# Activations transposed by VectorE and carried through DRAM, in place of TensorE transposes: an attention and mixer block on one core

## The chip, the core and the metric

The kernel runs on one core of a Trainium2 chip. The core has five engines, each with its own instruction stream: TensorE (PE) for matmuls, VectorE (DVE), ScalarE (ACT), GpSimd (POOL) and SyncE (SP), which here issues the DMAs. Data is computed on in SBUF (128 partitions); matmuls write PSUM. DRAM is reached by DMA. The metric is the device time of one execution in microseconds; the median of three runs of the kernel before is 1322.94 us (1322.71 to 1323.16).

## The reference

x has S = 2048 tokens of D = 576 channels, F = 4608 is the hidden width. Attention (32 heads of 18 channels, each token looking at itself and seven tokens at steps of two before it) and a mixer block both read the normalized x, and are added to x.

```python
def _A_ref(x, wqkv, wo):
    qkv = transpose((x @ wqkv).reshape(B, S, 3, H, Dh), 2, 0, 3, 1, 4)
    ...
    attn = _softmax(logits, axis=-1)
    o = einsum("bhsw,bhswd->bhsd", attn, vg)
    return transpose(o, 0, 2, 1, 3).reshape(B, S, D) @ wo

def _B_ref(x, w1, w2, w3, w4):
    h = _gelu(_layernorm(x) @ w1)
    ...                       # four channel groups shifted by +1, -1, +2, -2 tokens
    hs = concatenate([g0, g1, g2, g3], axis=-1) @ w2
    x1 = x + hs
    h2 = _gelu(_layernorm(x1) @ w3) @ w4
    return x1 + h2

xn = _layernorm(x)
return x + _A_ref(xn, wqkv, wo) + _B_ref(xn, w1, w2, w3, w4)
```

## The kernel before

**Matmuls.** Operands are split into two parts of a shorter float format, hi and lo (ACT rounds to hi, DVE subtracts to get lo). A product over 576 channels is 14 matmuls (`PAIRS`, L35): three for each of four chunks of 128 channels (hi·hi, hi·lo, lo·hi), and two for the last 64 channels, whose hi and lo share one chunk ("the tail"). An activation block that PE reads is thus `xt` of shape 128 x 9 x 512: channel on the partition, nine slices (0 to 3 hi, 4 the tail with hi in rows 0 to 63 and lo in rows 64 to 127, 5 to 8 lo), 512 tokens. Two such blocks live in `ring`, two more in `xp`.

**Transposing.** Layernorm and residual work has the token on the partition (16 tiles of 128 tokens, `Y[:, t, :]`), so each tile must be turned. `transposes` (L97) does it: four PE transposes (L102) of 128 x 128, for every second tile one more for two tiles' tails (L105), into a PSUM tile of the pool psb; ACT copies hi out (L107, L110), DVE makes lo (L111, L114). It is called for the normalized x (`prep_x`), for z, the layernorm of that again (`z_prep`, L146), for the layernorm of x1 (`n_prep`, L473), and for the attention output o (`prep_o`, L688).

**Stages, in PE's order.** Every engine runs its instructions in program order.
- Q: q, k, v for 16 tiles (`q_half`, L236), spilled to DRAM (`qkvd`).
- Mix (loop at L422): for each of four 512-token blocks b four tiles of W1 columns (`mix_tile`) and a remainder (`mix_rem`), whose 16-row groups are exchanged by eight small DMAs v<-u (L400, L401); pieces of work from `todo` then place them in T4 (L414). z of block b+1 is prepared meanwhile. W2 is loaded (`load_w2`, its tails by eight DMAs, L370) and split here.
- W2 (L481): 16 tiles; after each DVE adds to Y (L495) and takes statistics (`stats`: L88 to L90 on DVE, the power of -1/2 on POOL, L91). x1's layernorm of tiles 0 to 7 is prepared here, of 8 to 15 in units 0 to 2 (`LATE`, L645).
- The MLP: 72 units u = (c, b) of two hidden chunks and one block (L697). A unit is two `up` (14 matmuls, two gelus on ACT, lo on DVE) and four `down` of the unit before (12 matmuls, addition to Y on DVE, L639). `up` uses two PSUM buffers (psa), `down` three (psb). Attention runs in pieces on DVE in the background (`bg`) and stores o to DRAM (`od`, L554).
- The o stage (L743 to L767): the last four downs, then 16 tiles of o times Wo. o is read back two tiles at a time (`load_o`), turned and split one tile at a time.

All DMAs are issued by SP in program order, and an instruction whose data are not ready holds those behind it.

## Time and profile before

| | |
|---|---|
| median of three runs | 1322.94 us |
| the profiled execution | 1322.94 us |
| its span in the trace | 1321.2 us |
| DMA, share of 16 engines | 24%, 92.6 MB |
| under 512 B | 73504 of 120325 packets |
| granted TensorE clock | 1.0 |

The profile is of one execution. The span runs from the first to the last record; "busy" is an engine's time in instructions. A group row gives a program line, engine, operation, tiles and shapes, its count, then busy time and mean duration of one in ns, then idle time before. A row of a timeline gives start and length in us.

### The profile page before, as it was taken

What the parts mean: (1) busy time and instruction counts of PE and PEld (TensorE: products, weight loads), DVE (VectorE), ACT (ScalarE), POOL (GpSimd) and SP (SyncE); (2) the same over time, 40 slices, a digit from 0 to 9 for tenths busy, and PEclk for the clock granted to TensorE, in tenths of its full rate; (3) what the DMA queues carried; (4) which work ended last, traced back from release to release, by engine and by line L of the source; (5) the groups of instructions that cost most, each with busy time, mean ns of one, the idle gap of its engine ahead of it and who ended that gap; (6) DMA issues with size and microseconds to landing.
All of it is one profiled execution on the core that took longest, in us unless ns stands there. A gap on an engine that the chain in (4) does not pass through costs nothing.

```text
span 1321.2 us, 18855 instructions
## 1 busy us (share of the span) xinstructions
PE 1312.1 (99%) x7894; PEld 1208.0 (91%) x7894; DVE 921.9 (70%) x1332; ACT 348.2 (26%) x633; POOL 35.2 (3%) x92
## 2 busy tenths in 40 slices
PE   8999999999999999999999999999999999999998
PEld 8999998899899999999999999999999999999998
DVE  6443326687676778878868868878877886884454
ACT  4322225411423222222122222223213223122111
POOL 2010100011000000000000000000000000000000
PEclk9999999999999999999999999999999999999999
DMA  7644322020112021221221220220320200212164
GB/s 211 152 107 108 98 68 69 18 82 28 59 30 80 20 71 39 71 71 39 71 71 29 80 71 20 90 71 20 90 71 19 82 28 20 71 42 95 46 192 140
DMA packets 120325, 93.76 MB, mean 71 GB/s; under 512 B 73504, under 2 KB 100000, under 8 KB 120240
## 3 DMA queue, kind: packets, MB, share of 16 engines
q1 hardware_dynamic: 120240, 92.56, 23.9%
q8 instruction: 62, 1.02, 0.3%
q14 instruction: 23, 0.19, 0.0%
HBM read 67.83 MB, written 23.66 MB: 69 GB/s over the span
## 4 chain that ended last, share of the span: by engine, by line
PE 96%; DVE 2%; ACT 1%; SPq 1%; issue 1%; DMA 0%; POOL 0%; DVEq 0%; ACTq 0%; POOLq 0%
PE ps L636 34%; PE p L616 34%; PE ps L133 18%; PE ps L230 3%; PE p L380 3%; PE ps L102 2%; PE p L272 0%; PE p L395 0%; PE p L764 0%; DVE bn L88 0%; PE ps L105 0%; ACT xt L107 0%; DVE xt L111 0%; SPq L370 0%; DVE xt L114 0%
## 5 line engine op out<-in xcount | busy, mean ns | idle before, releaser
L636 PE MATMUL ps<-W,hi 128*128 128x288 f32 x2304 | 397.9, 294 | 0.5 <-DVE oT L114 0.5
L636 PEld LDWEIGHTS ps<-W,hi 128*128 128x128 f32 x2304 | 339.5, 188 | 6.1 <-PE ps L102 0.7
L620 ACT ACTIVATE hi<-p 128x512 fp32r<-128x512 f32 x144 | 86.2, 599 | 619.3 <-PE p L616 619.3
L636 PE MATMUL ps<-W,lo 128*128 128x288 f32 x1152 | 245.3, 294 | 0.0
L616 PE MATMUL p<-xt,W 128*128 128x512 f32 x1008 | 235.4, 390 | 0.0
L616 PE MATMUL p<-x1n,W 128*128 128x512 f32 x1008 | 234.9, 389 | 0.0
L622 DVE TENSOR_TENSOR lo<-g,hi 128x512 fp32r<-128x512 f32 x144 | 99.7, 692 | 193.2 <-ACT g L621 193.2
L639 DVE TENSOR_TENSOR Y<-ps,Y 128x576 f32<-128x576 f32 x288 | 212.8, 751 | 16.3 <-PE ps L636 16.1
L616 PEld LDWEIGHTS p<-x1n,W 128*128 128x128 f32 x1008 | 187.2, 188 | 36.8
L616 PEld LDWEIGHTS p<-xt,W 128*128 128x128 f32 x1008 | 187.1, 188 | 36.9
L636 PEld LDWEIGHTS ps<-W,lo 128*128 128x128 f32 x1152 | 185.4, 187 | 0.0
L133 PE MATMUL ps<-WQ,xt 128*128 128x432 f32 x672 | 135.3, 360 | 0.0
L133 PEld LDWEIGHTS ps<-WQ,xt 128*128 128x128 f32 x672 | 125.2, 188 | 5.2
L111 DVE TENSOR_TENSOR xt<-ps,xt 128x512 fp32r<-128x512 f32 x40 | 27.6, 689 | 87.2 <-ACT xt L110 52.1
L568 DVE TENSOR_TENSOR prod<-q,k 128x1152 f32<-128x1152 f32 x64 | 86.5, 1351 | 0.0
L571 DVE TENSOR_REDUCE L<-prod 128x64 f32<-128x1152 f32 x64 | 86.2, 1347 | 0.0
L621 ACT ACTIVATE g<-p 128x512 f32<-128x512 f32 x144 | 85.4, 593 | 0.0
L548 DVE TENSOR_TENSOR prod<-v,L 128x1152 f32<-128x1152 f32 x56 | 75.6, 1350 | 0.0
L552 DVE TENSOR_TENSOR o<-o,prod 128x1152 f32<-128x1152 f32 x56 | 75.6, 1350 | 0.0
L118 ACT CAST W<-rawf 128x640 fp32r<-128x640 f32 x72 | 50.5, 702 | 68.9 <-PE ps L636 62.2
L133 PE MATMUL ps<-Wo,oT 128*128 128x288 f32 x420 | 59.1, 298 | 0.2
L133 PEld LDWEIGHTS ps<-Wo,oT 128*128 128x128 f32 x420 | 56.2, 188 | 1.4 <-issue 1.4
(103 smaller groups left out, 941.9 us busy)
## 6 DMA issues: line engine op xcount, KB each, us to landing
qkvd<-stg SPq DMA_DIRECT2D x24, 432.0 KB, 3.4
rawf<-in_B_w_dram SPq DMA_DIRECT2D x36, 288.0 KB, 3.0
rawf<-in_B_w_dram SPq DMA_DIRECT2D x36, 256.0 KB, 2.9
xin<-in_A_x_dram SPq DMA_DIRECT2D x16, 288.0 KB, 3.8
q<-qkvd SPq DMA_DIRECT2D x8, 576.0 KB, 3.8
k<-qkvd SPq DMA_DIRECT2D x8, 576.0 KB, 5.7
v<-qkvd SPq DMA_DIRECT2D x8, 576.0 KB, 5.9
od<-o SPq DMA_DIRECT2D x8, 576.0 KB, 4.9
```

The source lines that it names most:

```text
L118: act.copy(dst_hi, raw)
L133: pe.matmul(ps[:, h, :n], xs(a), ws(b, h), start=i == 0, stop=i == len(PAIRS) - 1)
L548: dve.tensor_tensor(dst, vv, Lf[:, :, w:w + 1].to_broadcast([128, TPP * GH, HD]), op=ALU.mult)
L552: dve.tensor_tensor(o, o, dst, op=ALU.add)
L568: dve.tensor_tensor(prod.rearrange("p (j h) d -> p j (h d)", h=GH), q, k[:, r0:r0 + TPP, :], op=ALU.mult)
L571: dve.tensor_reduce(Lf[:, :, w], prod, axis=AX.X, op=ALU.add)
L616: pe.matmul(ps, W3[f][:, w, :], x1n[b][:, a, :], start=n == 0, stop=n == len(PAIRS) - 1)
L620: act.activation(hi, ps, AF.Gelu_apprx_tanh)
L621: act.activation(g32, ps, AF.Gelu_apprx_tanh)
L622: dve.tensor_tensor(lo, g32, hi.bitcast(F32), op=ALU.subtract)
L636: pe.matmul(ps[:, k, :HF], h[:, col], w[:, p, k * HF:(k + 1) * HF], start=n == 0, stop=n == len(seq) - 1)
L639: dve.tensor_tensor(yv, ps[:, :, :HF], yv, op=ALU.add)
```

## The change

z, the layernorm of x1, and o are no longer transposed by PE. Per tile, `turn` lets DVE transpose 32 x 32 pieces into a buffer `ST` (512 channels in one instruction, the 64 of the tail twice in another). After four tiles `put` writes ST to DRAM by four DMAs, one for every 32 partitions, such that rows come to lie by channel; `get` reads the block into the slices 4 to 8 of `xt` by two DMAs; `split_x` makes hi and lo of it (ACT and DVE). Columns of a block then lie in another order of tokens (32-token groups first), which the gelus undo by reading PSUM in a permuted order (`in_order`, `by_token`); o is read from DRAM in the matching order (`quads`), four tiles at a time into one buffer.

The work is put at other places: z is turned in Q after second halves of tiles 6 to 13; its blocks are fetched and split at tiles 12 and 14, at the end of Q, and within mix; x1's layernorm (its norm now on POOL) is turned at W2's tiles 2 to 5, 9, 10, 13 and 14 and, for the last four tiles, in unit 0. Its blocks are fetched at tiles 8 and 13 and in units 0 and 1, and split at tiles 11 and 15 and in units 1 and 2. o is turned after the downs of units 68 to 71, fetched from unit 69 on, and split in units 70 and 71, after the last downs, and at tile 5 of the o stage. The attention is finished one unit earlier (u = 67). In mix, matmuls write PSUM tiles of psb instead of psa, block 3 starts with its remainder, and the loads and splits of W2 and the pieces of `todo` come at other steps.

```diff
...
-    def norm(dst, src, kind, t):
-        dve.tensor_scalar(dst, src, MV[kind][:, t, 0:1], RS[kind][:, t, 1:2],
+    def norm(dst, src, kind, t, eng=dve):
+        eng.tensor_scalar(dst, src, MV[kind][:, t, 0:1], RS[kind][:, t, 1:2],
                           op0=ALU.subtract, op1=ALU.mult)
 
...
@@ -114,6 +112,53 @@
...
+    def room(p):
+        nonlocal ST, RT
+        ST = p.tile([128, 20, 128], F32, name="st")
+        RT = p.tile([128, 512], F32R, name="rt")
+
+    def turn(src, t):
+        c = slice(32 * t, 32 * t + 32)
+        dve.transpose(ST[:, 4:20, c], src[:, :512].rearrange("p (j c) -> p j c", c=32))
+        dve.transpose(ST[:, 0:4, c].rearrange("p (a j) c -> p a j c", a=2),
+                      src[:, 512:].rearrange("p (j c) -> p j c", c=32)[:, None, :, :]
+                      .to_broadcast([128, 2, 2, 32]))
+
+    def put(key):
+        xd[key] = dram.tile([5, 128, 512], F32, name="xd", bufs=4)
+        for q in range(4):
+            sp.dma_start(dram_ap(xd[key], 128 * q, [[512, 32], [32 * 512, 20], [1, 128]]),
+                         ST[32 * q:32 * q + 32])
+
+    def get(key, xt):
+        for k in ((0, 3), (3, 5)):
+            sp.dma_start(xt[:, 4 + k[0]:4 + k[1], :].bitcast(F32),
+                         xd[key][k[0]:k[1]].rearrange("k p c -> p k c"))
+
+    def split_x(xt, part=None):
+        raw = xt.bitcast(F32)
+        if part != 1:
+            act.copy(RT[64:128, :], raw[64:128, 4, :])
+            act.copy(xt[0:64, 4, :], raw[0:64, 4, :])
+            dve.tensor_tensor(xt[64:128, 4, :], raw[64:128, 4, :], RT[64:128, :].bitcast(F32),
+                              op=ALU.subtract)
+        for h in range(2) if part is None else (part,):
+            hi, lo = slice(2 * h, 2 * h + 2), slice(2 * h + 5, 2 * h + 7)
+            act.copy(xt[:, hi, :], raw[:, lo, :])
+            dve.tensor_tensor(xt[:, lo, :], raw[:, lo, :], raw[:, hi, :], op=ALU.subtract)
+
+    def in_order(blk):
+        return blk.rearrange("p (q t c) -> p t q c", q=4, t=4)
+
+    def by_token(blk):
+        return blk.rearrange("p (t q c) -> p t q c", q=4, t=4)
+
+    def quads(t_, b, q):
+        return dram_ap(t_, (512 * b + 128 * q) * D, [[D, 32], [32 * D, 4], [1, D]])
+
...
@@ -137,15 +182,12 @@
...
+    room(w1pool)
+
+    def z_turn(t):
+        z = w1pool.tile([128, D], F32, name="z", bufs=1)
+        norm(z, Y[:, t, :], 1, t)
+        turn(z, t % 4)
 
...
@@ -238,6 +280,8 @@
...
+        if t == NT - 1 and h == 1:
+            get(("z", 1), ring_block(("z", 1)))
         spill(stg, t, 2 * h * CG, 2 * CG)
 
...
@@ -333,18 +377,17 @@
...
-                if t >= NT - 2:
-                    z_prep(2 * (t - NT + 2) + 1)
-                    z_norm(2 * (t - NT + 2) + 3)
                 if t in (5, 6):
                     split_w1(t - 5)
-            else:
-                if t == NT - 4:
-                    z_norm(0)
-                    z_norm(1)
-                if NT - 3 <= t < NT - 1:
-                    z_prep(2 * (t - NT + 3))
-                    z_norm(2 * (t - NT + 3) + 2)
+                if t == 12:
+                    get(("z", 0), ring_block(("z", 0)))
+                if t == 14:
+                    split_x(xring["z", 0])
+            elif 6 <= t < 14:
+                z_turn(2 * t - 12)
+                z_turn(2 * t - 11)
+                if t % 2:
+                    put(("z", (t - 7) // 2))
...
@@ -375,27 +422,27 @@
 
     def mix_tile(b, m):
         xt = xring[("z", b)]
-        ps = psa.tile([128, 512], F32, name="p1", tag="a")
+        ps = psb.tile([128, 2, 512], F32, name="ps", tag="b")[:, 0, :]
         for i, (a, w) in enumerate(PAIRS):
             pe.matmul(ps, W1[:, w, m * 128:(m + 1) * 128], xt[:, a, :],
                       start=i == 0, stop=i == len(PAIRS) - 1)
...
         c = 2 + b * 512
         hi = H[0][m][:, c:c + 512]
-        act.activation(hi, ps, AF.Gelu_apprx_tanh)
-        act.activation(g32, ps, AF.Gelu_apprx_tanh)
+        act.activation(by_token(hi), in_order(ps), AF.Gelu_apprx_tanh)
+        act.activation(by_token(g32), in_order(ps), AF.Gelu_apprx_tanh)
...
     def mix_rem(b):
         xt = xring[("z", b)]
-        ps = psa.tile([128, 512], F32, name="p1", tag="a")
+        ps = psb.tile([128, 2, 512], F32, name="ps", tag="b")[:, 0, :]
         for a in range(9):
             pe.matmul(ps, W1R[:, a if a < 5 else a - 5, :], xt[:, a, :], start=a == 0, stop=a == 8)
...
-        act.copy(u, ps)
+        u = mupool.tile([128, 512], F32, name="u", bufs=2)
+        v = mupool.tile([128, 512], F32, name="v", bufs=2)
+        act.copy(by_token(u), in_order(ps))
...
@@ -417,26 +464,27 @@
...
     todo = []
-    w2raw[0] = load_w2(0)
-    w2raw[1] = load_w2(1)
     for b in range(NB):
-        for i, m in enumerate((0, 1, 2, 4, 3)):
-            nz = 4 * (b + 1) + i
+        if 0 < b < NB - 1:
+            get(("z", b + 1), ring_block(("z", b + 1)))
+        for i, m in enumerate((0, 1, 2, 4, 3) if b < 3 else (4, 0, 1, 2, 3)):
             if m < 4:
                 mix_tile(b, m)
             else:
                 todo += mix_rem(b)
-            if b + 1 < NB and i < 4:
-                z_prep(nz)
-                if nz + 2 < NT:
-                    z_norm(nz + 2)
-            if todo and (i in (1, 2) or len(todo) > 5):
+            if b + 1 < NB and i in (1, 2):
+                split_x(xring["z", b + 1], i - 1)
+            for _ in range((0, 1, 1, (1, 2, 2, 2, 3)[i])[b]):
                 todo.pop(0)()
-            k = {(0, 1): 0, (0, 2): 1, (0, 4): 2, (1, 4): 3, (2, 4): 4}.get((b, i))
+            if b == 0 and i < 2:
+                w2raw[i] = load_w2(i)
+            k = {(0, 4): 0, (1, 1): 1, (1, 4): 2, (2, 1): 3, (2, 4): 4}.get((b, i))
             if k is not None:
                 split_w(W2[:, k, :], W2[:, 5 + k, :], w2raw[k])
                 if k < 3:
                     w2raw[k + 2] = load_w2(k + 2)
...
@@ -466,22 +514,19 @@
 
     x1n = {}
 
...
+    def n_turn(t, zpool):
+        z = zpool.tile([128, D], F32, name="rz", tag="rz")
+        norm(z, Y[:, t, :], 2, t, pool)
+        turn(z, t % 4)
+        if t % 4 == 3:
+            put(("n", t // 4))
 
...
+    nsp = tc.tile_pool(name="nsp", bufs=1, reuse_waits="tile")
+    room(nsp.__enter__())
     for t in range(NT):
         ps = psb.tile([128, 2, 512], F32, name="ps", tag="b")
-        if 6 <= t < 14:
-            n_norm(t - 6, mpool)
...
@@ -499,10 +544,19 @@
...
-        if 6 <= t < 14:
-            n_prep(t - 6)
-        if 2 <= t and todo:
-            todo.pop(0)()
+        if 2 <= t < 6:
+            n_turn(t - 2, rzpool)
+        if t in (9, 10, 13, 14):
+            k = {9: 4, 10: 6, 13: 8, 14: 10}[t]
+            n_turn(k, rzpool)
+            n_turn(k + 1, rzpool)
+        if t in (8, 13):
+            x1n[t // 13] = ring_block(("n", t // 13))
+            get(("n", t // 13), x1n[t // 13])
+        if t in (11, 15):
+            split_x(x1n[t // 15])
...
@@ -642,9 +698,8 @@
     NU = len(units)
     RATE = [5.9, 5.9, 5.9, 5.9]
     wop = None
-    LATE = {(0, 0): (8, 9), (0, 1): (10, 11), (1, 0): (12,), (1, 1): (13,), (2, 0): (14,), (2, 1): (15,)}
+    LATE = {(0, 0): (12, 13), (0, 1): (14, 15)}
...
-    otile, xagain = {}, {}
-
-    def load_o(t):
-        if t % 2 == 0 and t < NT:
-            src = od[t * 128:(t + 2) * 128, :].rearrange("(a p) d -> p a d", a=2)
-            otile[t // 2] = opool.tile([128, 2, 512], F32, name="ot", bufs=2)
-            sp.dma_start(otile[t // 2], src[:, :, :512])
-            ztail[t // 2] = base.tile([128, 128], F32, name="ztail", bufs=2)
-            sp.dma_start(ztail[t // 2].rearrange("p (a c) -> p a c", a=2), src[:, :, 512:])
+    otile, xagain, xo = {}, {}, {}
+
+    def load_o(b):
+        if b < NB:
+            otile[b] = opool.tile([128, 4, D], F32, name="ot", bufs=1)
+            for q in range(4):
+                sp.dma_start(otile[b][32 * q:32 * q + 32], quads(od, b, q))
 
...
-    def prep_o(t):
-        if t >= NT:
-            return
-        oT[t] = opool.tile([128, 9, 128], F32R, name="oT", bufs=3)
-        o = otile[t // 2]
-        tail = (ztail[t // 2], [(oT[t - 1], 0), (oT[t], 0)]) if t % 2 else None
-        transposes(o[:, t % 2, :], tail, oT[t], 0)
-        dve.tensor_tensor(Y[:, t, :], Y[:, t, :], xagain[t], op=ALU.add)
+    def o_turn(b, t):
+        turn(otile[b][:, t, :], t)
+        if t == 3:
+            put(("o", b))
+
+    def o_block(b):
+        if b < 2:
+            xo[b] = ring_block(("o", b))
+        else:
+            xo[b] = xp.tile([128, 9, 512], F32R, name=f"x1n{b}")
+        return xo[b]
+
+    def add_x(t):
+        if t < NT:
+            dve.tensor_tensor(Y[:, t, :], Y[:, t, :], xagain[t], op=ALU.add)
 
...
         r = RATE[b] / 6 if u >= 3 else 0.0
-        if u == NU - 4:
+        if u == NU - 5:
             while not state["done"]:
                 bg(1e9)
             open_wo()
+            load_o(0)
+        if u == NU - 4:
             load_wo(0)
             load_wo(2)
         if u == NU - 3:
             split_wo(0)
             load_wo(4)
-            load_o(0)
-            load_o(2)
             load_xa(0)
             load_xa(1)
         if u == NU - 2:
@@ -719,18 +779,27 @@
             split_wo(4)
         for i in range(C):
             bg(r, False)
-            ts = LATE.get((u, i), ())
-            for t in ts:
-                n_norm(t, hp)
             up(c, b, i)
-            for t in ts:
-                n_prep(t)
+            for t in LATE.get((u, i), ()):
+                n_turn(t, tp)
+            if u < 2 and i == 1:
+                get(("n", u + 2), x1n[u + 2])
+            if u in (1, 2):
+                split_x(x1n[u + 1], i)
         if b == 3:
             split_w3(2 * c + 3)
         if prev is not None:
             for j in range(4):
                 bg(r, j == 1)
                 down(*prev, j)
+                if u >= NU - 4:
+                    o_turn(u - NU + 4, j)
+                if u >= NU - 2 and j == 1:
+                    split_x(xo[u - NU + 2])
+            if u >= NU - 4:
+                load_o(u - NU + 5)
+            if u >= NU - 3:
+                get(("o", u - NU + 3), o_block(u - NU + 3))
...
     for j in range(4):
         if j < 3:
-            prep_o(j)
+            add_x(j)
             load_xa(j + 2)
         down(*prev, j)
-    load_o(4)
+    split_x(xo[2])
 
     for t in range(NT):
+        b, s = divmod(t, 4)
...
+        if t == 1:
+            get(("o", 3), o_block(3))
+        if t == 5:
+            split_x(xo[3])
+
+        def oT(a, b=b, s=s):
+            return xo[b][:, a, s * 128:(s + 1) * 128]
+
         if t < NT - 1:
             ps = psb.tile([128, 2, 512], F32, name="ps", tag="b")
-            mm_tok(ps, lambda a, t=t: oT[t][:, a, :], lambda b, h: Wo[:, b, h * HF:(h + 1) * HF], HF)
-            prep_o(t + 3)
+            mm_tok(ps, oT, lambda b, h: Wo[:, b, h * HF:(h + 1) * HF], HF)
+            add_x(t + 3)
             load_xa(t + 5)
-            load_o(t + 6)
             dve.tensor_tensor(yv, ps[:, :, :HF], yv, op=ALU.add)
             sp.dma_start(of[t * 128:(t + 1) * 128, :], Y[:, t, :])
...
```

More of the change, by code (lines that the diff above doesn't have):

```diff
@@ L73, in tail_half @@
         if t % 2 == 0:
-            ztail[t // 2] = base.tile([128, 128], F32, name="ztail", bufs=2)
+            ztail[t // 2] = qpool.tile([128, 128], F32, name="ztail", bufs=2)
         return ztail[t // 2][:, t % 2 * 64:t % 2 * 64 + 64]
-    def norm_z(dst, kind, t):
-        norm(dst, Y[:, t, :512], kind, t)
-        norm(tail_half(t), Y[:, t, 512:], kind, t)
     def pair_tail(src, xts, t):
@@ L439, in fused_block @@
                     w2raw[k + 2] = load_w2(k + 2)
+    assert not todo
+    mup.__exit__(None, None, None)
     w1p.__exit__(None, None, None)
@@ L467, in fused_block @@
     x1n = {}
-    def n_norm(t, zpool):
-        zp[t] = zpool.tile([128, D], F32, name="rz", tag="rz", bufs=2)[:, :512]
-        norm_z(zp[t], 2, t)
-    def n_prep(t):
-        xt = x1n.get(t // 4)
-        if xt is None:
-            xt = x1n[t // 4] = ring_block(("n", t // 4))
-        transposes(zp[t], pair_tail(ztail[t // 2], xt, t), xt, (t % 4) * 128)
+    def n_turn(t, zpool):
[4 more added lines that the diff above has]
+            put(("n", t // 4))
     load_f(0)
     load_f(1)
+    nsp = tc.tile_pool(name="nsp", bufs=1, reuse_waits="tile")
+    room(nsp.__enter__())
     for t in range(NT):
         ps = psb.tile([128, 2, 512], F32, name="ps", tag="b")
-        if 6 <= t < 14:
-            n_norm(t - 6, mpool)
         def xs(a, t=t):
@@ L512, in fused_block @@
     hp = ctx.enter_context(tc.tile_pool(name="hp", bufs=2, reuse_waits="tile"))
+    tp = ctx.enter_context(tc.tile_pool(name="tp", bufs=1, reuse_waits="tile"))
+    room(tp)
     apc = tc.tile_pool(name="ap", bufs=1, reuse_waits="tile")
```

31 lines of the change are left out of this document (14 added, 17 removed).

## The prediction

> **What bounds the kernel now.** I read the head of the page, then the chain of work that ended last.
>
> ```profile
> span 1321.2 us, 18855 instructions
> PE 1312.1 (99%) x7894; PEld 1208.0 (91%) x7894; DVE 921.9 (70%) x1332; ACT 348.2 (26%) x633; POOL 35.2 (3%) x92
> PE 96%; DVE 2%; ACT 1%; SPq 1%; issue 1%; DMA 0%; POOL 0%; DVEq 0%; ACTq 0%; POOLq 0%
> PE ps L636 34%; PE p L616 34%; PE ps L133 18%; PE ps L230 3%; PE p L380 3%; PE ps L102 2%; PE p L272 0%; PE p L395 0%; PE p L764 0%; DVE bn L88 0%; PE ps L105 0%; ACT xt L107 0%; DVE xt L111 0%; SPq L370 0%; DVE xt L114 0%
> ```
>
> TensorE (PE) is busy for 99% of the span and makes 96% of the chain; its transposes (L102) are in the chain with 2%. So time comes off only by taking work from PE, and only if nothing then makes PE wait. The profiled execution is the median itself: 1322.94 us, 1.7 more than its span; I work from 1322.9.
>
> The second reading is by stage: a stage's length, then the busy time of PE, PEld, DVE, ACT and POOL.
>
> ```profile
> 196.80:263.90 67.10, 66.28 (x315) 54.12 (x314) 43.09 (x80) 35.40 (x71) 0.76 (x18) 1.00 0.16 42
> 263.90:328.30 64.40, 63.88 (x485) 63.21 (x484) 51.35 (x120) 11.45 (x24) 10.43 (x15) 1.00 0.17 49
> 328.30:365.20 36.90, 36.49 (x219) 32.03 (x218) 25.53 (x51) 13.30 (x30) 2.09 (x9) 1.00 0.19 67
> 1250.20:1321.20 71.00, 67.55 (x509) 66.07 (x507) 34.89 (x59) 10.55 (x27) 0.00 (x0) 1.00 0.52 167
> ```
>
> These are mix, W2, the first three units, and the o stage: exactly where the change works. DVE is at 51.35 of 64.40 us in W2, the least room of the four. GB/s, the last column, shows DMA nearly idle in the first three.
>
> **What the change removes.** The timeline of PE gives the start and length of each run of matmuls:
>
> ```profile
> 263.92 3.34 PE L133 MATMUL ps<-W,h 128*128 128x288 f32 x24
> 267.62 3.35 PE L133 MATMUL ps<-W,h 128*128 128x288 f32 x24
> 1254.41 3.96 PE L133 MATMUL ps<-Wo,oT 128*128 128x288 f32 x28
> 1263.09 3.96 PE L133 MATMUL ps<-Wo,oT 128*128 128x288 f32 x28
> ```
>
> From 263.92 to 267.62 one tile of 28 matmuls takes 3.71 us undisturbed. From 1254.41 to 1263.09, two tiles with two sets of transposes (eight L102, one L105) take 8.68. A pair of sets costs 8.68 - 7.42 = 1.25.
>
> ```profile
> L102 PE MATMUL ps<-ident,z 128*128 128x128 f32 x64 | 9.6, 272 | 0.0
> L102 PE MATMUL ps<-ident,rz 128*128 128x128 f32 x64 | 9.6, 276 | 0.9 <-DVE rz L94 0.7
> L102 PE MATMUL ps<-ident,ot 128*128 128x128 f32 x64 | 9.6, 272 | 0.0
> ```
>
> 64 transposes of each kind are 16 sets, so 24 pairs go: **-30.0 us**. W2 confirms the price (64.40 less 16 x 3.71 = 5.0 for eight sets). The transposes' own durations, 9 x 0.27 = 2.4 a pair, overlap each other and the matmuls beside them, so I count the steps between starts, not the busy time. Lower end: 24, if a pair were worth 1.0.
>
> **What it adds, and its prices.** Per tile, VectorE (DVE) now does a turn of two StreamTransposes, which no row shows. Nearest rows:
>
> ```profile
> L111 DVE TENSOR_TENSOR xt<-ps,xt 128x512 fp32r<-128x512 f32 x40 | 27.6, 689 | 87.2 <-ACT xt L110 52.1
> L119 DVE TENSOR_TENSOR W<-rawf,W 128x640 fp32r<-128x640 f32 x36 | 29.6, 822 | 0.0
> L119 DVE TENSOR_TENSOR Wo<-rawf,Wo 128x1152 fp32r<-128x1152 f32 x2 | 2.7, 1350 | 0.0
> L107 ACT CAST xt<-ps 128x512 fp32r<-128x512 f32 x40 | 23.7, 592 | 36.3 <-PE ps L105 19.8 <-PE ps L102 16.4
> L639 DVE TENSOR_TENSOR Y<-ps,Y 128x576 f32<-128x576 f32 x288 | 212.8, 751 | 16.3 <-PE ps L636 16.1
> L620 ACT ACTIVATE hi<-p 128x512 fp32r<-128x512 f32 x144 | 86.2, 599 | 619.3 <-PE p L616 619.3
> L414 DVE SCALAR_TENSOR_TENSOR T<-v,sgn,u 32x512 fp32r<-32x512 f32 x16 | 11.9, 746 | 0.6
> L94 DVE TENSOR_SCALAR Y<-xin,mv,rs 128x576 f32<-128x576 f32 x16 | 9.3, 578 | 6.5 <-POOL rs L91 6.4
> ```
>
> A turn writes 512 + 128 elements per partition; I take 0.95 us (0.69 for 512, about 0.26 for 128; ends 0.82, one instruction of 640, and 1.9, double). A split of a block is on ACT two copies of 512 and two of 1024 (1.2 + 2 x 1.0), on DVE one subtraction of 512 and two of 1024 (0.69 + 2 x 1.2 = 3.1). Gelus that now read PSUM permuted stay at 0.60 (ends 0.60 and 1.2): ACT has slack in every stage, so even 1.2 would lie beside PE.
>
> Norms of x1 go to GpSimd (POOL):
>
> ```profile
> 292.23 0.55 POOL L91 TENSOR_TENSOR rs<-rs,mhalf 128x1 f32<-128x1 f32 x1 [2.40 <-DVE rs L90]
> 331.39 0.79 POOL L518 MEMSET mask<- 128x512 f32 x1
> 312.15 0.76 DVE L495 TENSOR_TENSOR Y<-ps,Y 128x576 f32<-128x576 f32 x1 [0.94 <-PE ps L133]
> 314.12 0.69 DVE L111 TENSOR_TENSOR xt<-ps,xt 128x512 fp32r<-128x512 f32 x1
> ```
>
> The pow takes 0.55; a 128x512 memset 0.79; for a 128x576 norm I estimate 1.15 (ends 0.8 and 1.6). The Trainium skill, GPSIMD Engine Reference, § 3.1, gives at best 769 ns per 512 elements, which by it would make 0.87 here, and the sum 3 us less; no run shows it yet. Between 312.15 and 314.12 DVE adds a W2 tile to Y and takes its statistics: 2.0.
>
> Each of 12 blocks goes through DRAM: a put of four DMAs (1.31 MB), a get of two (0.79 and 0.52 MB).
>
> ```profile
> 211.97 0.59 SPq L400 DMA_DIRECT2D v<-u  x1
> 217.08 3.76 SPq L370 DMA_DIRECT2D rz<-in_B_w_dram  x8
> v<-u SPq DMA_DIRECT2D x32, 32.0 KB, 2.0
> od<-o SPq DMA_DIRECT2D x8, 576.0 KB, 4.9
> 330.00:336.00 6.00, 5.93 (x31) 4.66 (x29) 5.13 (x13) 2.48 (x7) 2.09 (x9) 1.00 0.89 318
> 1184.70:1190.00 5.30, 5.30 (x42) 5.30 (x42) 3.32 (x5) 1.70 (x3) 0.00 (x0) 1.00 0.77 203
> 1185.33 20.29 SPq L663 DMA_DIRECT2D rawf<-in_A_wo_dram  x2
> ```
>
> The SyncE queue (SP) issues in order, one DMA per 0.64: eight v<-u DMAs run from 211.97 to 217.08, then eight rz loads 3.76. A small DMA lands 2.0 after issue. Five loads at 330 us moved 318 GB/s at 0.89 busy; the od store, in pieces of 288 bytes, 203. I take 2.0 us + bytes / 330 GB/s, end 203.
>
> **Q stage: nothing added.** From the page's 40 slices of 33 us:
>
> ```profile
> DVE  6443326687676778878868868878877886884454
> ```
>
> In slices 3 to 6 (66 to 198 us), where the sixteen z turns lie, DVE is busy for 20 to 40%. Two tiles' norms (0.58 each, row L94) and turns add 3.1 us to each x tile's two halves, some 11.4 us, of which DVE has at least 7 to spare; without that room 16 x 1.5 = 24 would stand on the path. Puts and get z0 overlap the tiles that follow.
>
> **Mix: +3.8 (0 to 7).** Count from the start of the stage. Without its twelve sets it lasts 67.1 - 7.5 = 59.6, a block (four tiles of 14 matmuls, a remainder of 9) 14.9, the remainder 2.1. That of b=1 ends at 26.6; its copy on ACT, behind a gelu pair and copies of a split, lets v<-u be issued from 29.3 to 34.3. Behind that on SP stand W2's load of the tails (to 38.2) and get z3, which b=3 needs. Its first part lands at 38.2 + 2.0 + 2.4 = 42.6. The second half of its split follows ACT's gelus of b=2's third tile (46.9) and, on DVE, their subtraction and a T4 placing: it ends at 50.1. b=3 opens with the remainder, which reads all nine slices and so ends at 50.6, not 46.8. Lower end 0, if the copy of b=1 is early by 3; upper 7, if transfers go at 203. Get z1 and z2 have 10 us and more in hand.
>
> **W2: +18 (9 to 25).** Here DVE becomes the bound. From the end of mix it has: late placing of T4 (two blocks, 0.75 per group) 7; 16 x 2.0 = 32; 12 turns, 11.4; w splits 3; two x1n splits 6. Each turn also waits on POOL, since pow and norm follow that tile's statistics in POOL's order: four single turns wait 0.55 + 1.15 + 0.2 = 1.9 each, four pairs 2.1, together 16. Sum 75, less about 1 that overlaps: 74 against PE's 59.4. Then
> - unit 0's ups run to 65.8, unit 1 reads the second half of x1n1 from 67.1 and gets it at 74: 6.9;
> - the four late turns follow (POOL waits and two lo's between them) and end at 81.6. SP then holds put n3 and behind it get n2: 1.31 + 0.79 MB give 81.6 + 0.6 + 2.0 + 6.4 = 90.6. The split of x1n2 stands in DVE's order ahead of the first addition of a down, about 94.8. With three PSUM buffers the fourth down waits for that addition; it would have started at 83.8. Another 11.
> Queued behind are the attention loads and get n3; unit 3 is reached at 109, n3 lands by 104: nothing more. Lower end 9: turns and norms at their cheap ends leave some 7 and the get about half.
>
> **o stage: +18.4 (12 to 35).** One tile buffer for o makes a loop: four turns, put, load_o of the next block behind it, four turns. The timeline of PE gives a unit:
>
> ```profile
> 1190.88 6.52 PE L616 MATMUL p<-xt,W 128*128 128x512 f32 x28
> 1197.23 0.69 PE L636 MATMUL ps<-W,hi 128*128 128x288 f32 x4
> 1203.58 6.52 PE L616 MATMUL p<-xt,W 128*128 128x512 f32 x28
> ```
>
> Two ups last 6.35, four downs 6.35, a unit 12.7. The loop needs (1.31 + 1.18) MB / 330 = 7.5, + 2.0, + four turns and the three additions between them 6.0 = 15.5: 2.8 more than a unit, each time. From u=67 = 0: block 0's turns end at 27; put o0 stands on SP behind the second Wo load, which waits for a w split (row 1185.33: 20 us of waiting now) until 28.1. Wo's 0.59 MB, put and load: o1 lands at 39.4, wanted 34.2. Its turns end 45.3; o2 lands 54.8. Then in u=70 the split of block 0 waits for its get, issued behind both (3.8 MB: 45.3 + 13.5 = 58.8); the addition behind it on DVE ends at 62.5, and u=71's downs need it. o2's turns end 65.2, o3 lands 74.7, and the same happens with the split of block 1: addition at 82.4. PE's last downs, due at 69.8, end at 88.2. In the final tiles xo2's split stops DVE to 98, but three PSUM buffers hide that but for 0.1. Lower end 12 with a put and load of 7.5; upper 35 at 203 GB/s.
>
> **Sum:** 1322.9 - 30.0 + 3.8 + 18 + 18.4 = **1333**.
>
> **The rivals.**
> - *Everything is hidden (faster).* For: DMA is nearly idle through mix and W2, and downs have three PSUM buffers. Against: the o loop exceeds a unit already at 330 GB/s. If put and load overlapped so that they lasted 7.5 and turns cost 0.82, the loop is 13.0, and cheap turns and norms bring W2's DVE to 65: 1322.9 - 30 + 6 (W2) + 1 (o) = 1300. It decides at a loop of 12.7.
> - *Only the o loop stalls.* POOL norms at 0.8 and waits partly hidden bring DVE to PE's pace, W2 loses 4: 1322.9 - 30 + 4 + 16 = 1313.
> - *Transfers of 32 partitions run slowly.* Each put and load_o DMA covers a quarter of the partitions; the od store shows that 203 GB/s occurs. Loop 12.3 + 2.0 + 6.0 = 20.3, 4.8 more for three blocks and 4 for W2: 1333 + 20 = 1353. Against: four of them run together. The Trainium skill, SBUF — State Buffer, § Door 1: The DMA port swizzle, states 189 GB/s at 1 MiB for partitions 0 to 31 and 328 for all 128, and under "Can I just issue two DMAs to hit both halves?" that two together gain 6%; its 189 would make it 1356. No transfer of the trace has this form and size.
> - *The turn costs double* (1.9, a write in 32-column pieces, which no row shows): 0.95 more for the 16 of W2 and the 12 of the o loop: 1333 + 26 = 1359.
> - *The change doesn't do what it says*: some sets stay. The diff leaves only x's (L102 ps<-ident,Y); no chance given.
>
> **How the numbers follow.** Forecast 0.50 (own range 1318 to 1348), all hidden 0.12, only the o loop 0.14, slow transfers 0.16, double turn 0.08. Range: 1306 to 1358, which leaves out the first rival and the top of the last. A difference under 0.2% (2.6 us) can't be told from none. Below 1320.3: 0.12 + 0.12 of the o-loop case + 0.03 of the forecast's low end = 0.27; within: 0.06; slower: 0.67.
>
> **What would show it.** L102 keeps 64 rows. PE's idle before L616 in units 1 and 2, and before L636 in u=71 and the last downs, with DVE as releaser, is the forecast; a get (DMA) landing later than 2 us + bytes / 330 is the slow rival. Turn rows near 0.95 in all, POOL norms near 1.15, DVE busy or waiting on POOL through all of W2. Wrong if PE has no idle stretch over 3 us: then 1300.

## The result, and the profile after

The changed kernel takes 1385.38 us (median of four runs, 1384.72 to 1387.3) where the kernel before takes 1322.86: ratio 1.0475, 95% interval 1.0457 to 1.0493. It is slower, as forecast, but by 62.5 us in place of 10, and above the range.

The head of the page and the chain that ended last (SPq and the like stand for an engine's sequencer, issue for time in which no wait shows):

```profile
span 1383.2 us, 18484 instructions
PE 1303.1 (94%) x7678; PEld 1198.1 (87%) x7678; DVE 935.5 (68%) x1320; ACT 348.5 (25%) x585; POOL 75.4 (5%) x108
PE 79%; DVE 6%; DMA 5%; POOL 3%; SPq 3%; ACT 2%; issue 2%; DVEq 0%; POOLq 0%; ACTq 0%
```

PE has 216 matmuls less, nine for each of 24 pairs of sets, but is busy only 9 us less (1303.1 after 1312.1), for some of the others ran slower. Its share of the chain fell from 96% to 79%; DVE, DMA, POOL and SP took its place. By stage (length, then busy time of PE, PEld, DVE, ACT and POOL, granted clock, DMA share, GB/s): mix, W2, units 0 to 2, units 68 to the last downs, the final tiles:

```profile
194.75:258.36 63.61, 60.76 (x261) 49.25 (x261) 34.81 (x47) 36.02 (x59) 0.76 (x18) 0.97 0.37 110
258.36:326.32 67.96, 61.95 (x450) 61.01 (x449) 44.08 (x101) 8.08 (x12) 27.93 (x23) 0.97 0.39 96
326.32:393.82 67.50, 35.72 (x182) 30.94 (x181) 29.45 (x49) 16.64 (x26) 23.48 (x18) 0.77 0.47 139
1220.13:1311.25 91.12, 65.75 (x354) 59.30 (x353) 42.37 (x71) 18.05 (x28) 0.00 (x0) 0.83 0.64 152
1311.25:1383.20 71.95, 61.79 (x450) 61.31 (x448) 29.14 (x39) 6.26 (x8) 0.00 (x0) 0.95 0.53 167
```

Against the kernel before: mix 63.6 us after 67.1, W2 68.0 after 64.4, units 0 to 2 67.5 after 36.9, units 68 to the last downs 91.1 after 59.3, the final tiles 72.0 after 71.0; the stretches not shown differ by 2.0 less (Q) and 0.6 more. Two places hold the loss: from the start of W2 to unit 2, and from unit 68 on. Note the granted clock of units 0 to 2 and from unit 68 on, 0.77 and 0.83, where it was 1.00 before. In the timeline of PE the waits are in brackets, with what ended them:

```profile
294.94 4.98 PE L178 MATMUL ps<-W,h 128*128 128x288 f32 x24 [1.84 <-DVE Y L540]
300.28 3.33 PE L178 MATMUL ps<-W,h 128*128 128x288 f32 x24
343.85 7.73 PE L672 MATMUL p<-xt,W 128*128 128x512 f32 x26 [9.09 <-DVE xt L151]
377.87 1.33 PE L692 MATMUL ps<-W,hi 128*128 128x288 f32 x4 [21.53 <-DVE Y L695]
1274.13 1.33 PE L692 MATMUL ps<-W,hi 128*128 128x288 f32 x4 [5.83 <-DVE Y L695]
1298.19 1.30 PE L692 MATMUL ps<-W,hi 128*128 128x288 f32 x4 [12.08 <-DVE Y L695]
1322.04 14.15 PE L178 MATMUL ps<-Wo,xt 128*128 128x288 f32 x89 [6.93 <-DVE Y L695]
```

294.94 is a tile of W2, 343.85 unit 1's up, 377.87 the fourth down of unit 1, 1274.13 and 1298.19 downs behind additions that DVE holds, 1322.04 a final tile. The ups and downs wait where the prediction put a wait, but longer; for the waits in W2 and in the final tiles it had none. All of PE's waits over 0.3 us add up to 38 us in W2 and units 0 to 2 and 32 from unit 68 on.

The price rows, the time from issue to landing, and three windows in which only puts, only the load of o, and only a get move:

```profile
L125 DVE STREAM_TRANSPOSE st<-rz 128x512 f32<-128x512 f32 x16 | 11.4, 712 | 37.6 <-POOL rz L92 37.6
L126 DVE STREAM_TRANSPOSE st<-rz 128x128 f32<-128x128 f32 x16 | 4.3, 270 | 0.0
L92 POOL TENSOR_SCALAR rz<-Y,mv,rs 128x576 f32<-128x576 f32 x16 | 39.3, 2463 | 3.3 <-DVE st L126 3.3
L151 DVE TENSOR_TENSOR xt<-xt 128x1024 fp32r<-128x1024 f32 x16 | 19.1, 1221 | 5.3 <-ACT xt L150 5.2
xd<-st SPq DMA_DIRECT2D x48, 320.0 KB, 5.9
1258.50:1261.20 2.70, 1.11 (x8) 1.11 (x9) 1.54 (x3) 0.00 (x0) 0.00 (x0) 1.00 0.93 177
1266.00:1269.00 3.00, 2.30 (x11) 1.56 (x9) 0.00 (x0) 0.00 (x0) 0.00 (x0) 1.00 0.96 214
1272.00:1274.00 2.00, 0.00 (x0) 0.00 (x0) 1.47 (x3) 0.00 (x0) 0.00 (x0) 0.53 1.04 386
```

The loop of o, in SP's and DVE's timelines: puts and gets of SP with their issue time, a load of x (L739), and the first turns of blocks 2 and 3 with their waits:

```profile
1256.95 4.18 SPq L133 DMA_DIRECT2D xd<-st  x4
1281.71 4.17 SPq L133 DMA_DIRECT2D xd<-st  x4
1310.20 3.57 SPq L138 DMA_DIRECT2D x1n<-xd  x2
1313.87 12.92 SPq L739 DMA_DIRECT2D xa<-in_A_x_dram  x4
1272.53 0.71 DVE L125 STREAM_TRANSPOSE st<-ot 128x512 f32<-128x512 f32 x1 [12.49 <-DMA ot<-od]
1296.50 0.71 DVE L125 STREAM_TRANSPOSE st<-ot 128x512 f32<-128x512 f32 x1 [12.30 <-DMA ot<-od]
```

Block 1's turns end as put o1 begins (1256.95), and block 2 is there at 1272.5, 15.6 later; the next leg, 1281.7 to 1296.5, takes 14.8. From first turn to first turn pass 24.0, nearly two units of 12.7. The load of x's tile 2 is issued at 1313.87, behind get o2 and, before that, put o3 (1305.96), which waits for block 3's turns.

A turn costs 0.71 + 0.27 = 0.98, as estimated. The norm on POOL takes 2.46 us, the estimate was 1.15 with an end of 1.6; DVE's turns of x1 wait 37.6 us for it in total. A put's DMA lands after 5.9 us in the median. While only puts move (1258.5 on) the rate is 177 GB/s with the DMA engines busy for 0.93; while only the load of o moves (1266 on) 214, not 330. A get, which covers all 128 partitions in pieces of 2 KB, moves at 386 (1272 on).

### The profile page after: what moved, and what is told of

Its sections match the earlier page's. It is cut to its first block, busy times and chain, and to the rows that moved or that the text cites. A ratio compares the mean times of both kernels' runs of the same rounds, so it can differ in the third digit from the quotient of the medians.

```text
span 1383.2 us, 18484 instructions
## 1 busy us (share of the span) xinstructions
PE 1303.1 (94%) x7678; PEld 1198.1 (87%) x7678; DVE 935.5 (68%) x1320; ACT 348.5 (25%) x585; POOL 75.4 (5%) x108
## 4 chain that ended last, share of the span: by engine, by line
PE 79%; DVE 6%; DMA 5%; POOL 3%; SPq 3%; ACT 2%; issue 2%; DVEq 0%; POOLq 0%; ACTq 0%
PE p L672 30%; PE ps L692 30%; PE ps L178 14%; POOL rz L92 3%; PE ps L272 3%; DMA xt<-xd 2%; SPq L133 1%; PE ps L427 1%; DVE st L125 1%; SPq L734 1%; DVE T L461 1%; DVE Y L695 1%; DVE bn L86 1%; DMA x1n<-xd 1%; DVE Y L540 1%
## 5 line engine op out<-in xcount | busy, mean ns | idle before, releaser
L692 PE MATMUL ps<-W,hi 128*128 128x288 f32 x2304 | 404.4, 297 | 47.3 <-DVE Y L695 47.2
L692 PEld LDWEIGHTS ps<-W,hi 128*128 128x128 f32 x2304 | 345.0, 191 | 55.3 <-DVE Y L695 37.7
L692 PE MATMUL ps<-W,lo 128*128 128x288 f32 x1152 | 248.2, 297 | 0.0
L672 PE MATMUL p<-xt,W 128*128 128x512 f32 x1008 | 236.6, 391 | 10.2 <-DVE xt L151 9.1
L672 PEld LDWEIGHTS p<-x1n,W 128*128 128x128 f32 x1008 | 187.5, 188 | 36.9
L692 PEld LDWEIGHTS ps<-W,lo 128*128 128x128 f32 x1152 | 188.3, 190 | 0.0
L178 PE MATMUL ps<-W,h 128*128 128x288 f32 x384 | 55.4, 301 | 6.0 <-DVE Y L540 6.0
L178 PEld LDWEIGHTS ps<-W,h 128*128 128x128 f32 x384 | 53.3, 193 | 7.0 <-DVE Y L540 6.9
L164 DVE TENSOR_TENSOR W<-rawf,W 128x640 fp32r<-128x640 f32 x72 | 56.4, 785 | 0.0
```

The lines of the kernel that those rows point to most:

```text
L164: dve.tensor_tensor(dst_lo, raw, dst_hi.bitcast(F32), op=ALU.subtract)
L178: pe.matmul(ps[:, h, :n], xs(a), ws(b, h), start=i == 0, stop=i == len(PAIRS) - 1)
L672: pe.matmul(ps, W3[f][:, w, :], x1n[b][:, a, :], start=n == 0, stop=n == len(PAIRS) - 1)
L692: pe.matmul(ps[:, k, :HF], h[:, col], w[:, p, k * HF:(k + 1) * HF], start=n == 0, stop=n == len(seq) - 1)
```

## The experiments

Times are medians; ratios are to the kernel before in the same runs. The theory after the result: (1) the norm on POOL sets W2 and the first units; (2) put and load_o are slow because each DMA covers 32 partitions, and the o loop holds three waits one inside the other (load, put, get with its split); (3) a load of x has come to stand behind a put and a get; (4) PE runs at half rate after waits. The rivals: bytes or the queue set the transfers; the loss comes from the way itself, wherever it is used.

**The norm back on VectorE.**

```diff
-        norm(z, Y[:, t, :], 2, t, pool)
+        norm(z, Y[:, t, :], 2, t)
```

> The layernorm of x1 goes back from GpSimd to VectorE (128x576, some 0.58 us each); nothing else. If the norm on GpSimd (2.30 to 2.46 us, and VectorE waiting 2.95 for each single turn and 2.95 + 1.37 for each pair) sets W2 and the first units, W2's 12 turns lose 4 x 2.4 + 4 x 3.2 = 22 us of VectorE's time and the four late turns about 8, and of the 34 us by which W2 and units 0 to 2 are longer some 20 to 28 go: about 1361. If put and get alone decide there, the turns were only early or late in waiting for them: less than 6 us go.

Measured: 1361.56 us (1.0289, 1.0272 to 1.0306), 23.8 less. What is left in its timeline of PE between W2 and unit 2:

```profile
327.69 6.19 PE L672 MATMUL p<-xt,W 128*128 128x512 f32 x26 [1.05 <-DVE xt L151]
354.84 1.33 PE L692 MATMUL ps<-W,hi 128*128 128x288 f32 x4 [16.20 <-DVE Y L695]
```

No wait in W2, 1.05 at unit 1's up, and 16.2 at the fourth down: put n3, get n2 and the split. So theory 1 holds, for W2 and for part of unit 1.

**The loads of o by token tile.**

```diff
-            for q in range(4):
-                sp.dma_start(otile[b][32 * q:32 * q + 32], quads(od, b, q))
+            for s in range(4):
+                sp.dma_start(otile[b][:, s, :], dram_ap(od, (512 * b + 32 * s) * D,
+                                                        [[128 * D, 4], [D, 32], [1, D]]))
```

> The four loads of a block of o are cut by token tile (each over all 128 partitions, pieces of 2304 B as before) in place of by quarter of the partitions; nothing else. If a DMA over 32 partitions is slow by its form, the 1.18 MB move near the 318 GB/s that five 128-partition loads showed in the kernel before, instead of some 205: the leg from a block's last turn to the next block's landing (15.6 and 14.8 us in the changed kernel) falls by about 2, three times, and the time to about 1379. If the rate is set by the bytes, the pieces or the one queue, the leg stays within 0.5 us and the time at 1385.

Measured: 1407.94 us (1.0642, 1.0626 to 1.0658), worse by 22.6, which neither theory had. In a window in which only such a load moves:

```profile
1256.00:1262.00 6.00, 3.98 (x20) 3.98 (x21) 3.10 (x6) 0.00 (x0) 0.00 (x0) 0.72 0.26 99
```

0.26 of the DMA engines are busy, at 99 GB/s: this form, whose outermost dimension is 4, seems to reach only four of the 16 engines, as 0.26 is near 4/16. The run tells nothing about partitions.

**The same loads, 128 successive tokens each.**

```diff
-            for q in range(4):
-                sp.dma_start(otile[b][32 * q:32 * q + 32], quads(od, b, q))
+            for s in range(4):
+                sp.dma_start(otile[b][:, s, :], od[512 * b + 128 * s:512 * b + 128 * s + 128, :])
```

> The four loads of a block of o each take 128 successive tokens over all 128 partitions (pieces of 2304 B, as before) in place of a quarter of the partitions; tokens of a block then come out in another order within the block, so the output has rows of the attention part exchanged; the work is the same. If 32 partitions are the slow form, 1.18 MB take 3.4 us in place of 5.9, the leg from last turn to landing (15.2) falls by 2.5, three times: about 1378. If bytes or the queue set the rate, the time stays within 2 us of 1385.

Measured: 1379.53 us (1.0429, 1.0413 to 1.0444). The pieces are the same 2304 B. The tokens of a block come in another order and nothing puts them back, so the output has rows of the attention part exchanged: the kernel serves to measure only. SP's put of block 1 and load of block 2, DVE's first and third turn after them, and a window in which only such a load moves:

```profile
1254.05 4.17 SPq L133 DMA_DIRECT2D xd<-st  x4
1258.27 4.47 SPq L734 DMA_DIRECT2D ot<-od  x4
1264.21 0.71 DVE L125 STREAM_TRANSPOSE st<-ot 128x512 f32<-128x512 f32 x1 [7.08 <-DMA ot<-od]
1275.14 0.70 DVE L125 STREAM_TRANSPOSE st<-ot 128x512 f32<-128x512 f32 x1
1263.00:1265.50 2.50, 2.50 (x13) 2.07 (x12) 1.29 (x3) 0.00 (x0) 0.00 (x0) 1.00 0.96 247
```

From the end of block 1's turns (1254.1) to the first turn of block 2 pass 10.1 us, where the changed kernel has 15.6. This is not all due to the form: cut by token tile, the first turn waits for one load of the four only. The last of the four lands 13.5 us after block 1's turns (1267.6 by its landing in the trace), in the changed kernel 15.4 (1272.3). So the form is worth some 1.9 us in this leg, a little less than the 2.5 expected, at 247 GB/s in place of 214; even over 128 partitions these loads don't reach 330. The early first turn bought little: the third turn starts at 1275.1, 9 us after the second, since the split between them waits for its get. A shorter wait uncovers the next. In all the time fell by 5.9.

**The put wide, the get narrow.**

```diff
-            sp.dma_start(dram_ap(xd[key], 128 * q, [[512, 32], [32 * 512, 20], [1, 128]]),
-                         ST[32 * q:32 * q + 32])
+            sp.dma_start(xd[key][k[0]:k[1]].rearrange("k p c -> p k c"),
+                         ST[:, 4 * k[0]:4 * k[1], :].rearrange("p (k j) c -> p k (j c)", j=4))
...
+            sp.dma_start(xt[32 * j:32 * j + 32, 4:9, :].bitcast(F32).rearrange("p k (q c) -> p (k q) c", q=4),
+                         dram_ap(xd[key], 128 * j, [[512, 32], [32 * 512, 20], [1, 128]]))
```

> The put is cut by channel chunk (two DMAs over 128 partitions, pieces of 2 KB) and the get by quarter of the partitions (four DMAs, pieces of 512 B), the other way round from the changed kernel; bytes are the same. If form sets the rate, the put takes 4.1 us of transfer in place of 7.5 and the get 7.5 in place of about 4: the o loop (put, then load) falls by about 3 three times, the splits of o wait for their gets longer, and W2's last put and get together stay; about 1378. If the bytes or the queue set it, put and get keep their times and the total stays within 3 us of 1385.

Measured: 1398.45 us (1.0573, 1.0557 to 1.0588), 13 worse. The put alone, the get alone, then DVE's turns around the split:

```profile
1266.80:1268.80 2.00, 1.42 (x11) 1.18 (x9) 2.00 (x4) 0.00 (x0) 0.00 (x0) 1.00 1.02 378
1278.00:1280.00 2.00, 0.00 (x0) 0.00 (x0) 1.40 (x3) 0.00 (x0) 0.00 (x0) 1.00 1.23 175
1280.07 0.69 DVE L125 STREAM_TRANSPOSE st<-ot 128x512 f32<-128x512 f32 x1
1290.10 0.70 DVE L125 STREAM_TRANSPOSE st<-ot 128x512 f32<-128x512 f32 x1
```

The put moves 378 GB/s in place of 177, the get 175 in place of 386. So the form sets the rate, for writes and reads alike, not the bytes or the queue. Which part of the form isn't shown: with the partitions (32 or 128) the pieces change too (512 B or 2 KB), and the loads of o, whose pieces stayed the same, gained only 214 to 247 from the partitions. The time rose because the get is now the narrow one and the third turn waits until 1290.1 for its split. The expectation named that wait, but not that it stands in the loop.

**The loads of x.** A third buffer, x's tile 2 loaded in unit 69, get o2 after the last downs and its split at tile 2.

> In the changed kernel the load of x for token tile 2 stands on the SyncE queue behind the last put and a get that waits for it, and TensorE waits 6.9 us for the addition. Here a third buffer lets it be loaded two units earlier, and the get of o's block 2 is issued after the last downs and its split moved to tile 2. If that queue order is the whole cause, 6 to 7 us go: about 1379. If the wait only passes on to the split of block 2 or to the additions of later tiles, the time stays at 1383 to 1385.

Measured: 1375.19 us (1.0395, 1.038 to 1.0411). 10.2 less, more than expected: the wait of 6.9, and about 3 of half rate (from 1270 on PE works 20 us at a granted clock of 0.50 in the changed kernel, 14 here).

**The loop of o, opened in two places.** First only the load a unit ahead, into a block that is free by then:

```diff
...
+                blk = o_block(b - 1).rearrange("p a c -> p (a c)")[:, :4 * D]
+                otile[b] = blk.bitcast(F32).rearrange("p (t d) -> p t d", d=D)
...
+        if u >= NU - 4:
+            load_o(u - NU + 5)
...
```

> The load of o's next block goes into a block of SBUF that is free by then (where its turned form comes later) and is issued after the ups, a down ahead of the put; the loop of put and load is opened. If the one buffer is what makes the loop (24.5 us from last turn to last turn where a unit has 12.7), it falls to some 19, in which the split waits for its get: about 1368. If the transfers' sum (put, load and get of a block, about 17 us) is what decides, the wait moves to the get and the time stays above 1378.

Measured: 1375.22 us (1.0394, 1.0379 to 1.0411): 10.2 less, between the two. Then only the splits moved, those of blocks 2 and 3 to tiles 3 and 6:

```diff
-                if u >= NU - 2 and j == 1:
-                    split_x(xo[u - NU + 2])
...
+        if j == 1:
+            split_x(xo[0])
+    split_x(xo[1])
...
```

> The splits of o's blocks 0 and 1 no longer stand between the second and the third turn of units 70 and 71; they come in the last downs and after them, those of blocks 2 and 3 at tiles 3 and 6. If a split that waits for its get is one part of the o loop, the step from last turn to last turn (24.5 us) falls to the 15.2 of put and load plus some 6: 7 us less in two units, of which some comes back as a wait of the first tiles for their splits: 1376 to 1381. If the wait for the load hides the split's, no change.

Measured: 1378.2 us (1.0415, 1.0401 to 1.043), 7.2 less. Both:

> Loads of o a unit ahead (the edit of the run with loads ahead) and the late splits together. What is left of the loop is that the one buffer of turned data must be written out before the next turns: about 9.5 us from the last turn, plus the turns 6 = 15.5, against a unit of 12.7. If put, load and get each hold the loop in turn, opening two of them gives more than the sum of each alone: 1360 to 1367. If DMA's total is the limit, 1372.

Measured: 1363.28 us (1.0306, 1.0292 to 1.032), 22.1 less, more than 10.2 + 7.2. DVE's first turns of blocks 2 and 3:

```profile
1264.42 0.71 DVE L125 STREAM_TRANSPOSE st<-xt 128x512 f32<-128x512 f32 x1 [5.72 <-DMA xd<-st]
1278.69 0.71 DVE L125 STREAM_TRANSPOSE st<-x1n 128x512 f32<-128x512 f32 x1 [6.51 <-DMA xd<-st]
```

They wait for the put (xd<-st) now: 14.3 from one to the next, against 24.0 in the changed kernel and 12.7 for a unit. So load, put and the get with its split had each held the loop; opening two leaves the put.

**PE kept busy through the wait.** 80 unused matmuls ahead of unit 1's fourth down:

```diff
+                if u == 1 and j == 3:
+                    fill = psa.tile([128, 512], F32, name="p1", tag="a")
+                    for _ in range(80):
+                        pe.matmul(fill, W3[0][:, 0, :], x1n[0][:, 0, :], start=True, stop=True)
```

> In unit 1 of the changed kernel, ahead of the fourth down that waits 21.5 us, TensorE does 80 matmuls (some 18 us) whose result is not used; the output is unchanged. If matmuls after a long wait run at half rate because TensorE stood still, the down after it takes 1.6 us in place of 3.05 and the next up starts at full rate: 1.5 to 2 us less, about 1383.5. If the slow matmuls come from something else (their operands, other engines), the down still takes about 3 us and the time stays.

Measured: 1383.41 us (1.0453, 1.0437 to 1.0469; runs from 1381.15 to 1386.47, so no difference is shown). The down, the up after it, the granted clock (the figure before the last two) during the unused matmuls and after the wait that is left, and last the clock in the changed kernel:

```profile
377.76 0.80 PE L692 MATMUL ps<-W,hi 128*128 128x288 f32 x4 [2.63 <-DVE Y L695]
379.69 7.91 PE L672 MATMUL p<-x1n,W 128*128 128x512 f32 x28
356.00:375.00 19.00, 19.00 (x88) 15.66 (x86) 3.25 (x5) 3.31 (x6) 3.10 (x9) 1.00 0.77 214
379.16:382.57 3.41, 3.41 (x11) 2.85 (x10) 1.49 (x2) 0.00 (x0) 0.00 (x0) 0.50 0.80 295
360.77:381.25 20.48, 3.38 (x13) 3.38 (x14) 5.83 (x8) 4.71 (x7) 0.00 (x0) 0.50 0.98 312
```

The down lasts 1.9 us (377.76 to 379.69), not 3.05; but the next pair of ups takes 7.9, where 6.5 is due. The slow stretch came later; it didn't go, and so the time shows nothing. The clock shows the cause: it stays at 1.00 while the unused matmuls run, where the changed kernel waits and has 0.50, and it falls to 0.50 behind the wait of 2.6 us that the filling left. So theory 4 holds: it is TensorE's standing still that lowers its clock.

**o back to TensorE.** The code of the kernel before for o, the rest as changed.

> Only o goes back: it is read, turned by TensorE and split tile by tile as in the kernel before; z and the layernorm of x1 stay as changed. From the start of unit 68 the changed kernel takes 163.1 us to the end of the span, the kernel before 130.3. If the o loop costs what it adds there and nothing before it depends on it, 32.8 go: about 1352.6. If half of that was the clock or the end of attention one unit earlier, 1360 or more.

Measured: 1353.54 us (1.0231, 1.0214 to 1.0248), 31.8 less: the loss from unit 68 on is o's own.

**Only where there is time.** z and x1's blocks 0 and 1 by the new way, norm on VectorE; x1's tiles 8 to 15 and o by TensorE, gelus of blocks 2 and 3 in plain order.

> Only z and the layernorm of x1's first two blocks take the new way, with the norm on VectorE; blocks 2 and 3 (tiles 8 to 15, in units 0 to 2) and o are turned by TensorE as before. If the way through DRAM costs only where a block is wanted at once, its gain stays: Q -2.0, mix -3.5 as in the changed kernel, W2 and the first units -5.0 plus at most 2 of VectorE's lag: 1312 to 1315, faster than before. If W2's lag comes from the turns and splits themselves and not from the norm on GpSimd, 1320 to 1326.

Measured: 1318.48 us (0.9966, 0.9953 to 0.9979), 3.5 above the end of the expected range. Two waits are left, before mix's last block and at unit 0:

```profile
242.07 0.73 PE L442 MATMUL ps<-xt,W1R 128*128 128x512 f32 x2 [3.12 <-ACT g L433]
324.84 1.62 PE L100 MATMUL ps<-ident,rz 128*128 128x128 f32 x8 [2.58 <-DVE rz L92]
```

They were the object of the next run, in which get z3 comes before the loads of W2's tails and x1's turns and get earlier:

```diff
+        if b == 2:
+            w2raw[4] = load_w2(4)
...
+        if 6 <= t < 10:
+            n_turn(t - 2, rzpool)
+        if t in (8, 12):
+            x1n[t // 12] = ring_block(("n", t // 12))
+            get(("n", t // 12), x1n[t // 12])
+        if t in (11, 14):
+            split_x(x1n[t // 14])
```

> The mixed kernel (z and x1's blocks 0 and 1 by the new way, the rest by TensorE) with two more moves: get z3 is issued ahead of the eight loads of W2's tails, and the turns and the second get of x1's layernorm come some tiles earlier in W2. If mix's 4 us of waiting are get z3 behind those loads (3.8 us of issuing), and 2.6 us at the start of the units are VectorE's lag from the late split, 1312 to 1315. If they come from ScalarE's and VectorE's own work, 1317 to 1319.

Measured: 1315.02 us (0.9944, 0.9931 to 0.9956), faster than both kernels, by 0.6% against the kernel before. Its waits:

```profile
239.66 0.73 PE L442 MATMUL ps<-xt,W1R 128*128 128x512 f32 x2 [0.60 <-ACT g L433]
323.06 1.94 PE L100 MATMUL ps<-ident,rz 128*128 128x128 f32 x8 [4.00 <-DVE rz L92]
```

Mix's wait for ACT fell from 3.12 to 0.60, so get z3 behind the eight loads was its cause. The one at unit 0 grew from 2.58 to 4.0, so the second move didn't help there.

## Why the prediction was right or wrong

The direction and most of the places were right. Four things were not: the price of the norm on POOL, the rate of the transfers, a queue in front of x, and TensorE's half rate after waits. Point by point, by its own steps:

- *What the change removes, 30.0.* Right in the main. Where nothing new waits most of it comes back: Q is 2.0 shorter, of 2.5 for its four sets, and the mixed kernel, which keeps 24 of the 48 sets' gain (half of 30 = 15), is 7.7 faster with about 6 of waits left in mix and unit 0.
- *Mix, +3.8.* Right: 67.1 - 7.5 + 3.8 = 63.4, measured 63.6, and its cause is shown by the last run.
- *The turn, 0.95; the split, 3.1.* Right: 0.98, and 0.69 + 2 x 1.22 = 3.1.
- *W2, +18 (9 to 25).* The order of the waits of units 0 to 2 was right, the size was not: without its 10.1 of removed sets the stretch was 101.3 - 10.1 = 91.2, and it is 135.5, so 44. The step that failed is "for a 128x576 norm I estimate 1.15 (ends 0.8 and 1.6)": 2.46. In W2 DVE waits 2.2 to 3.0 for a single turn and 4.3 for a pair, where the prediction had 1.9 and 2.1. So unit 1's up gets the second half of its block 85.5 us after W2's start, not at 74, and the late turns end at 100.6, not 81.6. A memset, which only writes, was no bound for an operation that reads a tensor and two columns of scalars. The run with the norm on VectorE took 23.8 off; this isn't a share of the 26 that were missing, since it holds waits that the prediction had counted. Put n3 and get n2 add about 4: the turns end at 358.9 and the split begins at 371.8 (from 363.4 on the chain shows 8.3 us of x1n<-xd), 12.9 in place of 9.0. The Trainium skill, GPSIMD Engine Reference, § 3.1, gives 769 ns at best for 512 elements, an estimate of 0.87 here; the measurement is 2.8 times that.
- *Transfers, "2.0 us + bytes / 330 GB/s, end 203".* Failed at the rate: 177 for puts, 214 for the load of o. With these a put and a load take 1.31 MB / 177 + 1.18 / 214 + 2.0 = 14.9 us, where the legs measured 15.6 and 14.8; so the term was built right and only its rate was off. The rival of 32 partitions said so with a chance of 0.16, though with 203 (its terms, 3 x 4.8 + 4, make 18, not 20). That the form of a DMA does it is shown (a put 378, a get 175 in the other form); whether the partitions or the pieces of 512 B do stays open for them, and for the loads the partitions alone gave 247 in place of 214. The Trainium skill, SBUF — State Buffer, § Door 1: The DMA port swizzle, has 189 GB/s for 32 partitions and 328 for 128; the puts' 177 and 378 fit, the loads' 214 and 247 don't show that step. Four DMAs at once on all quarters moved 177 together, so they didn't help, as that page's section on two DMAs lets one expect.
- *o stage, +18.4 (12 to 35).* From unit 68 on 163.1, where 130.3 less the sets' 10.0 was due: 43. Legs from last turn to landing were 15.6 and 14.8 in place of 9.5, steps from turn to turn 24 in place of 20. The loop itself was right, link by link: load, put, get with its split. And the prediction missed a queue: the load of x's tile 2, behind put o3 and get o2, 6.9 of waiting.
- *A term that was not there.* After waits PE is slow: from 294.94 a tile takes 5.34 where 3.71 is due, from 377.87 a down 3.05 where 1.59 is. The prediction put this at nothing without a reason. In the trace PE works 33 us at a granted clock of 0.50, which costs about 16. The sum: 73 of waits (38, 32 and 3 in mix) + 16 - 30 = 59, of the 62 that the span grew.
- *The chances.* Slower was right with 0.67. But each rival held one bad end. Here a dear norm on POOL, slow transfers, the queue in front of x and the half rate came together; the last two were in no case, and no case had two at once, so the range ended at 1358.

## What to carry to other kernels

Work taken off the bound engine is worth its time only where its replacement has slack: here z and half of x1's norm had it, o had none, and the same way is a gain of 0.6% in the mixed kernel and a loss of 5% where it is used throughout. When a loop of buffer, write, read and split is longer than its cover, every link counts, and shortening one shows the next; cost it link by link, with each DMA's partitions and pieces. An unseen operation on another engine wants a bound from a row that reads and computes, and where none exists, a wide end: the norm took three times the memset.

## What the runs showed of the hardware

- A wait can make what follows slow: while the granted clock is 0.50, PE matmuls take about twice as long (a group of four 1.33 us at 377.87 in place of 0.69). In the changed kernel's trace the spells at 0.50 last 3.41 us or a multiple (6.83, 10.24, 20.48), and all begin on one grid of 3.41. The first two rows are two windows of that grid in the changed kernel, the last two in the run with unused matmuls:

```profile
292.51:295.92 3.41, 1.57 (x12) 1.34 (x11) 2.52 (x6) 0.00 (x0) 0.79 (x1) 1.00 0.22 42
295.92:299.33 3.41, 3.41 (x16) 3.41 (x15) 3.24 (x10) 0.00 (x0) 1.11 (x2) 0.50 0.96 182
293.83:297.24 3.41, 1.75 (x13) 1.75 (x14) 3.25 (x8) 0.00 (x0) 0.46 (x2) 1.00 0.43 82
297.24:300.65 3.41, 3.41 (x28) 3.41 (x28) 3.20 (x11) 0.00 (x0) 0.68 (x2) 1.00 0.98 200
```

PE stood still for 1.84 us of the first window, and the next runs at 0.50; in the other run for 1.66 of one, after a wait as long, and the next runs at 1.00. The wait of 2.15 before 317.43 lies in two windows, 1.1 and 1.0, and nothing slows. So what counts seems to be whether PE stands still for about half of one window, not the length of a wait alone; this is inferred from these rows. The Trainium skill, TensorE: Matmul & The Clock Gate, § What's actually happening, tells of half the clock after an idle window of about 3.4 us and of 3.4 us to come back, on windows that run free; the lengths agree, but the tile at 294.94 was slow after a wait of only 1.84.
- A load with an outermost dimension of 4 moved 99 GB/s with 0.26 of the DMA engines busy; the same bytes by quarters of the partitions moved 214, and in plain order of all 128 partitions 247, the fastest of the three.
